# First block issued by a list schedule instead of a fixed table of slots

## Chip, cores and metric

The kernel runs on one core of one Trainium2 chip. The metric is the device time of one execution in microseconds (us). A core has TensorE (PE, products), VectorE (DVE), ScalarE (ACT) and GpSimd (POOL), each with an instruction queue of its own that it works off in order. SyncE (SP) issues nearly all DMA transfers, also in order. An instruction waits at the head of its queue until all that it needs is there.

## What is computed

An attention step in linear form, a gated unit and a second unit follow each other on 4608 tokens (8 batches of 576) of width 512, all in float32:

```
q_s = softmax(q, axis=d);  k_s = softmax(k, axis=s)      # per batch and head
x   = q_s @ (k_s^T @ v)                                  # (4608, 512)
y   = (silu(x @ w_gate) * (x @ w_val)) @ w_out           # d_ff = 1536
h   = y @ w_in;  solu = h * softmax(h)                   # d_ff = 1024
out = layernorm(solu) * g_ln @ w_out2
```

The weights arrive as 64-bit floats and are converted on the chip. Each product of two float32 matrices is made of three products of a high part and a low part (high x high, high x low, low x high).

## The kernel before

Tokens are worked on in nine blocks of 512. In a block the hidden width 1536 is cut into twelve groups n = 0 to 11. A group is a gate product g (12 matmuls, L753 to L755), a value product v (12) and an output product o (12) that adds to four accumulators y. After g comes a silu on ScalarE (L792); after v a multiplication on VectorE (L797), a cast to the high part ah on ScalarE (L800) and a subtraction to the low part al on VectorE (L801). o(n) needs ah and al. Four PSUM banks (gv) turn round among g, v and the small products of attention.

While block j runs, attention for block j+1 is made: row maxima of k (L399), maxima over all rows and subtraction (L411 to L432), exp (L493), k-v products (pk, L502) with reciprocals and two parts (L512 to L520), the q steps (L572 to L590, exp L580), q transposes (pq, L602) and x products (px, L666 to L668) with xh on ScalarE (L671) and xl on VectorE (L673).

The first block also converts all its weights. There are 18 raw tiles: wgv0 to wgv11 (gate and value columns of a group) and wo0 to wo5 (output rows of two groups). A conversion has four parts: two activations on ScalarE (L212, L213), two joins on VectorE (L221, L225), the cast to the high part on ScalarE (L236), and the low part on VectorE (L246). The joined result goes to a scratch tile t. Six raw tiles are loaded early, seven (mid: wgv4, wgv5, wo2, wgv6, wgv7, wo3, wgv8) into memory of the prologue, and the last five (again: wgv9, wo4, wgv10, wgv11, wo5) into slots of earlier weights. For these, the earlier weight must first have been used by its v product and stored to DRAM (stream_store, L258), from where later blocks load it again.

The prologue before the first block (attention of block 0 and the first four conversions) is ordered by a clock of nominal times (KEYS). In the first block, `first_tasks` puts every conversion and attention step at a fixed slot 3n to 3n+2 of the group n, and `block` issues slot after slot, each task with all its parts on all engines. So queues hold conversions in the order of use, one or two per group:

```
at(t, 3 * n, lambda no=no: conv_todo[no].start())
at(t, 3 * n + 2, lambda no=no, home=home: conv_todo[no].join(*home))
```

with the cast in the next group's first slot and the low part in its third. Where two conversions fall in one group, their scratch tiles are t2 and yt of the pool tmp. In the prologue they are two tiles t in the pool att0, whose memory the mid loads reuse. The conversions of blocks 1 to 8 are not there; those blocks reload converted weights.

Of the kernel before, what the change touches and what calls it, by code (L numbers as in the profile page):

```python
# [73 lines left out]
class Clock:  # L74
# [14 lines left out]
    def run(self):  # L89
        while self.todo:  # L90
            self.now, _, task = heappop(self.todo)
            if not task.done:
                d = task.step()
                if not task.done:
                    self.put(self.now + d, task)


def finish(f, *a):
# [3 lines left out]
def need(x):  # L102
    if not x:
        raise ValueError("an order that cannot be")
# [3 lines left out]
def attention_glu_solu_kernel(  # L108
# [46 lines left out]
    def f32(ap):  # L155
        return ap.bitcast(F32)
# [425 lines left out]
    def q_norm(pool, j, hs, eng=nc.gpsimd):  # L582
        qt = qt_t[j][1][:, :, hs, :]
        n, nc_, nh = qt.shape[:3]
        qs = stat.tile([n, nc_, nh, 1], F32, tag="qs", bufs=2, name="qs")
        nc.vector.tensor_reduce(out=qs[:, :, :, 0], in_=qt, axis=AX.X, op=ALU.add)
        nc.vector.tensor_scalar_add(out=qs, in0=qs, scalar1=1e-9)
        nc.vector.reciprocal(out=qs, in_=qs)
        q_step(j, hs, 3)
        eng.tensor_tensor(  # L590
            out=qt, in0=qt, in1=qs.to_broadcast([n, nc_, nh, D]), op=ALU.mult
        )
# [100 lines left out]
    def at(t, g, f, *a):  # L693
        t.setdefault(g, []).append((f, a))
# [52 lines left out]
    def y_of(j):  # L747
        return y_dram[:, :, BLOCKS[j][0]:sum(BLOCKS[j])]
# [46 lines left out]
    def v_rest(j, i, pv):  # L795
        st = acts[j, i]
        nc.vector.tensor_tensor(out=st, in0=st, in1=pv, op=ALU.mult)  # L797
        ah = apool.tile([P, BLOCKS[j][1]], F32R, tag="ah", bufs=2, name="ah")
        al = apool.tile([P, BLOCKS[j][1]], F32R, tag="al", bufs=2, name="al")
        nc.scalar.copy(out=ah, in_=st)  # L800
        nc.vector.tensor_tensor(out=al, in0=st, in1=f32(ah), op=ALU.subtract)  # L801
        acts[j, i] = (ah, al)

# [1 line left out]
        g_rest(j, i, proj("wg", j, i))  # L805

    def emit_v(j, i, *o):
        v_rest(j, i, proj("wv", j, i))
        pend.append((j, i, *o))

    def next_o(lag):
# [3 lines left out]
    def block(j, fs, dst, t, g0=0):  # L815

        r = {}
        for n, i in enumerate(fs):
            at(r, g0 + 3 * n, emit_g, j, i)
            at(r, g0 + 3 * n + 1, next_o, 1)  # L820
            at(r, g0 + 3 * n + 2, emit_v, j, i, n == 0, n == len(fs) - 1, dst)
        for g in sorted(r.keys() | t.keys()):
            for f, a in r.get(g, []) + t.get(g, []):
                finish(f, *a)
# [107 lines left out]
        load_w1(w_b, f"b{n}", *x)  # L932
    nc.sync.dma_start(out=g_sb, in_=g_ln.rearrange("(c p) -> p c", p=P))

    def first_tasks():

        t = {}
        later, first = [], conv_n[0]
        for n in range(NF - 1):
            for w, _, _ in later:
                at(t, 3 * n, w)
            for _, w, f in later:
                at(t, 3 * n + 2, w)
                if f in streamed:
                    at(t, 3 * n + 3, stream_store, f)  # L950
            later = []
            for m in range(2 - n % 2):
                if first == len(order):
                    break
                no, first = first, first + 1
                home = (tmp, ("t2", "yt")[m])
                at(t, 3 * n, lambda no=no: conv_todo[no].start())
                at(t, 3 * n + 2, lambda no=no, home=home: conv_todo[no].join(*home))
                nm, i = order[no]
                later.append((  # L960
                    lambda no=no: conv_todo[no].upper(), lambda no=no: conv_todo[no].rest(),
                    i if nm == "wgv" else None,
                ))
        need(first == len(order) and not later)
        for f in range(3):
            at(t, 0, stream_store, f)
        for n, (x, tag) in enumerate(zip(again, ("a0", "a1", "a3", "a4", "b0"))):
            at(t, 3 * n + 2, load_w1, w_b if tag == "b0" else wpool, tag, *x)
# [5 lines left out]
        for u in range(2):  # L974
            at(t, 20, kv_mm, ps_at, att, 1, 0, u)
        at(t, 21, kv_load, att, 1, HG)
        at(t, 21, v_load, att, 1, HG)
        at(t, 23, q_norm, att, 1, ALLH, nc.vector)
        at(t, 26, x_tiles, ph1x, 1)
        at(t, 29, kv_max_rows, att, 1, HG)  # L980
        at(t, 29, kv_max_all, att, 1, HG, HG)
        at(t, 30, kv_exp, 1, HG)
        for u in range(2):
            at(t, 32, kv_mm, ps_at, att, 1, HG, u)
        for p, (g, x) in enumerate(((26, 29), (27, 30), (30, 33), (31, 34))):
            at(t, g, q_transpose, ps_at, att, 1, p)
            at(t, x, x_mm, ps_at, 1, p)
        at(t, 33, kv_next, 1)
        at(t, 34, q_next, 1)
        for e, f in enumerate(STREAM):  # L990
            if f is not None and e > STREAM.index(None):
                at(t, 3 * f + 2, stream_next, 0, e)
        return t
# [277 lines left out]
```

## Time and profile before

| what | value |
|---|---|
| median of 3 runs | 1436.24 us (1435.14 to 1437.85) |
| the profiled execution | 1435.06 us, its span 1433.3 us |
| TensorE busy in the span | 1373.9 us (96%) |
| VectorE, ScalarE busy | 715.4 us (50%), 647.4 us (45%) |
| mean granted TensorE clock | 0.983 |
| first block (v0 to v11) | about 45 to 188 us |

A span is the time from the first to the last instruction. In a timeline each row gives start and duration; durations of matmuls overlap, so the time that one takes is the distance of starts. A bracket at a row's end gives the idle time of the engine before it and what ended it. A clock of 1.00 is 2.4 GHz, 0.5 is 1.2 GHz. In the list of waits, the engine on the left waited for what stands behind the arrow.

### The profile page before, as it was taken

What the parts mean: (1) busy time and instruction counts of PE and PEld (TensorE: products, weight loads), DVE (VectorE), ACT (ScalarE), POOL (GpSimd) and SP (SyncE); (2) the same over time, 40 slices, a digit from 0 to 9 for tenths busy, and PEclk for the clock granted to TensorE, in tenths of its full rate; (3) what the DMA queues carried; (4) which work ended last, traced back from release to release, by engine and by line L of the source; (5) the groups of instructions that cost most, each with busy time, mean ns of one, the idle gap of its engine ahead of it and who ended that gap; (6) DMA issues with size and microseconds to landing.
All of it is one profiled execution on the core that took longest, in us unless ns stands there. A gap on an engine that the chain in (4) does not pass through costs nothing.

```text
span 1433.3 us, 17363 instructions
## 1 busy us (share of the span) xinstructions
PE 1373.9 (96%) x6829; PEld 1135.1 (79%) x6829; DVE 715.4 (50%) x1227; ACT 647.4 (45%) x885; POOL 126.2 (9%) x106
## 2 busy tenths in 40 slices
PE   7886799999999999999999999999999999999998
PEld 5665588888888888888888888888878888888887
DVE  6776834434434434434444423331257666666663
ACT  4655425425424524524524514321147566566563
POOL 3000002102012012012021011000000000000000
PEclk8998899999999999999999999999999999999999
DMA  9971386475565565654645442562324433443341
GB/s 288 272 273 41 122 203 145 124 198 127 139 189 122 157 170 121 168 162 120 175 161 112 146 168 68 214 232 83 147 61 109 110 96 74 103 103 97 102 77 42
DMA packets 246657, 201.42 MB, mean 141 GB/s; under 512 B 204208, under 2 KB 218544, under 8 KB 234800
## 3 DMA queue, kind: packets, MB, share of 16 engines
q1 hardware_dynamic: 246576, 200.31, 49.9%
q8 instruction: 54, 0.88, 0.3%
q14 instruction: 27, 0.22, 0.1%
HBM read 140.51 MB, written 35.65 MB: 123 GB/s over the span
## 4 chain that ended last, share of the span: by engine, by line
PE 82%; DVE 7%; ACT 6%; SPq 2%; issue 2%; DMA 1%; ACTq 0%; DVEq 0%
PE wg L753 6%; PE wv L753 6%; PE wv L755 6%; PE wv L754 6%; PE y L753 6%; PE y L755 6%; PE y L754 6%; PE wg L754 6%; PE wg L755 6%; PE y L1166 4%; PE y L1165 4%; PE y L1164 4%; PE ph L1054 4%; PE ph L1053 4%; PE ph L1055 4%
## 5 line engine op out<-in xcount | busy, mean ns | idle before, releaser
L797 DVE TENSOR_TENSOR st<-st,wv 128x512 f32<-128x512 f32 x108 | 74.2, 687 | 354.5 <-PE wv L755 325.8
L800 ACT CAST ah<-st 128x512 fp32r<-128x512 f32 x108 | 66.8, 618 | 357.7 <-DVE st L797 357.6
L755 PE MATMUL wg<-xh,wgv 128*128 128x512 f32 x432 | 171.4, 397 | 9.1 <-DVE wgv L246 9.1
L753 PE MATMUL wg<-xh,wgv 128*128 128x512 f32 x432 | 173.2, 401 | 2.3 <-ACT xh L671 2.3
L753 PE MATMUL wv<-xh,wgv 128*128 128x512 f32 x432 | 169.3, 392 | 3.3 <-DVE xl L673 3.3
L754 PE MATMUL wg<-xl,wgv 128*128 128x512 f32 x432 | 170.8, 395 | 0.9 <-DVE xl L673 0.9
L755 PE MATMUL wv<-xh,wgv 128*128 128x512 f32 x432 | 168.9, 391 | 0.0
L754 PE MATMUL wv<-xl,wgv 128*128 128x512 f32 x432 | 168.8, 391 | 0.0
L753 PE MATMUL y<-ah,wo 128*128 128x512 f32 x432 | 168.8, 391 | 0.0
L755 PE MATMUL y<-ah,wo 128*128 128x512 f32 x432 | 168.3, 390 | 0.0
L754 PE MATMUL y<-al,wo 128*128 128x512 f32 x432 | 168.2, 389 | 0.0
L801 DVE TENSOR_TENSOR al<-st,ah 128x512 fp32r<-128x512 f32 x108 | 74.8, 693 | 92.0 <-ACT ah L800 92.0
L1166 PE MATMUL y<-w,zl 128*128 128x512 f32 (+1 forms) x296 | 113.8, 385 | 0.7 <-DVE zl L1135 0.7
L1164 PE MATMUL y<-w,zh 128*128 128x512 f32 (+1 forms) x296 | 113.8, 384 | 0.0
L1165 PE MATMUL y<-w,zh 128*128 128x512 f32 (+1 forms) x296 | 113.6, 384 | 0.0
L1053 PE MATMUL ph<-w,yh 128*128 128x512 f32 x288 | 113.0, 392 | 0.0
L1055 PE MATMUL ph<-w,yl 128*128 128x512 f32 x288 | 112.7, 391 | 0.0
L1054 PE MATMUL ph<-w,yh 128*128 128x512 f32 x288 | 112.6, 391 | 0.0
L755 PEld LDWEIGHTS wg<-xh,wgv 128*128 128x128 f32 x432 | 82.5, 191 | 28.3 <-DVE wgv L246 10.8
L792 ACT ACTIVATE st<-wg 128x512 f32<-128x512 f32 x108 | 64.4, 596 | 89.7 <-PE wg L755 89.4
L753 PEld LDWEIGHTS wg<-xh,wgv 128*128 128x128 f32 x432 | 82.7, 192 | 20.2 <-ACT xh L671 3.0
L753 PEld LDWEIGHTS wv<-xh,wgv 128*128 128x128 f32 x432 | 81.5, 189 | 20.2 <-DVE xl L673 3.5
(240 smaller groups left out, 2291.8 us busy)
## 6 DMA issues: line engine op xcount, KB each, us to landing
wgv<-w_dram SPq DMA_DIRECT2D x64, 1024.0 KB, 5.1
vt<-in_v_dram SPq DMA_DIRECT2D x64, 144.0 KB, 4.7
y_dram<-yt SPq DMA_DIRECT2D x9, 1024.0 KB, 4.4
yr<-y_dram SPq DMA_DIRECT2D x9, 1024.0 KB, 5.2
out_dram<-ot SPq DMA_DIRECT2D x35, 256.0 KB, 2.3
w_dram<-wgv SPq DMA_DIRECT2D x8, 1024.0 KB, 8.7
w_dram<-w2r SPq DMA_DIRECT2D x8, 1024.0 KB, 3.9
w<-w_dram SPq DMA_DIRECT2D x8, 1024.0 KB, 4.8
```

Of the source, the lines that this page charges most:

```text
L753: nc.tensor.matmul(out=po, lhsT=wh, rhs=rh, start=start, stop=False)
L754: nc.tensor.matmul(out=po, lhsT=wh, rhs=rl, start=False, stop=False)
L755: nc.tensor.matmul(out=po, lhsT=wl, rhs=rh, start=False, stop=stop)
L797: nc.vector.tensor_tensor(out=st, in0=st, in1=pv, op=ALU.mult)
L800: nc.scalar.copy(out=ah, in_=st)
L801: nc.vector.tensor_tensor(out=al, in0=st, in1=f32(ah), op=ALU.subtract)
L1053: nc.tensor.matmul(out=po, lhsT=yh[:, kk, s], rhs=wh, start=(kk == 0), stop=False)
L1054: nc.tensor.matmul(out=po, lhsT=yh[:, kk, s], rhs=wl, start=False, stop=False)
L1055: nc.tensor.matmul(out=po, lhsT=yl[:, kk, s], rhs=wh, start=False, stop=(kk == KD - 1))
L1164: nc.tensor.matmul(out=po[:, s], lhsT=zh[:, c, :], rhs=wh[:, s], start=first, stop=False)
L1165: nc.tensor.matmul(out=po[:, s], lhsT=zh[:, c, :], rhs=wl[:, s], start=False, stop=False)
L1166: nc.tensor.matmul(out=po[:, s], lhsT=zl[:, c, :], rhs=wh[:, s], start=False, stop=last)
```

## The change

`first_tasks` and the first call of `block` are replaced by `first_block`, which gives every step of the block to a planner (`Plan`): each task is a list of stages, each with an engine and a nominal time. The planner then simulates the engines on these times and issues a stage when it chooses it. Among the stages that could begin soon it takes that with the longest remaining chain, plus a number per task from a table of some hundred (`plan` in KEYS). A task's parts are now separated by `yield`, so parts of different tasks can interleave, and each conversion stands on its own. Only two conversions stay in the prologue's clock, and all later ones use t2 and yt. The tables say that mid loads land at 0, 2, 5, 12, 16, 23 and 27 us, that a store takes 0.5 us and lands 5 us later, and that a reload takes 1 us and lands 8 us later. Line numbers of the new kernel are higher by about 99.

```diff
     xmm=(23.65, 22.75, 25.3, 26.8),
-    conv=(17.35, 22.1, 26.0, 27.85),
+    conv=(17.35, 22.1),
+    mid=(0, 2, 5, 12, 16, 23, 27),
+    att1=(9, 40),
...
+class Plan:
+    PE, DVE, ACT, SP = 'PE DVE ACT SP'.split()
...
+    def add(self, name, stages, f, *a, after=(), at=0, behind=0, then=()):
...
+    def run(self, sizes):
...
+                    ready.append((begin, -rest((name, t["n"])) - self.first.get(name, 0), name))
+            need(ready)
+            begin, urgent, name = min(ready)
+            eng, us = (left[name]["stages"][left[name]["n"]][k] for k in ("eng", "us"))
+            for b, u, x in sorted(ready):
+                s = left[x]["stages"][left[x]["n"]]
+                if s["eng"] == eng and u < urgent and b < begin + max(us - self.patience, .1):
+                    begin, urgent, name, us = b, u, x, s["us"]
+            t = left[name]
+            s = t["stages"][t["n"]]
+            if s["slot"]:
+                took[s["slot"]].append(name)
+            table = s["table"] or table
+            free[s["eng"]] = begin + s["us"]
+            t["end"].append(begin + s["us"] + s["land"])
+            t["n"] += 1
+            t["task"].step()
...
+        return max(free.values())
...
+        yield d["km"]
...
-    def first_tasks():
...
-                at(t, 3 * n, lambda no=no: conv_todo[no].start())
-                at(t, 3 * n + 2, lambda no=no, home=home: conv_todo[no].join(*home))
...
-        at(t, 5, kv_max_rows, att, 1, 0)
-        at(t, 11, kv_max_all, att, 1, 0, HG)
-        at(t, 17, q_max, att, 1, ALLH, nc.vector)
-        at(t, 18, kv_exp, 1, 0)
-        at(t, 18, q_exp, 1, ALLH)
...
+    def first_block():
+        plan = Plan(*K["plan"])
+        PE, DVE, ACT, SP = plan.PE, plan.DVE, plan.ACT, plan.SP
...
+        def convert(no):
+            w = conv_todo[no]
+            w.start()
+            yield
+            w.join(*homes[turn[0] % 2])
+            turn[0] += 1
+            yield
+            w.upper()
+            yield
+            w.rest()
...
+            if no < 6:
+                after, t0 = (), 0
+            elif no < 13:
+                after, t0 = (), K["mid"][no - 6]
+            else:
+                after, t0 = (f"load{no}",), 0
+            plan.add(
+                f"w{no}", [(ACT, 2.4), (DVE, 2.5, 0, None, "t"), (ACT, 1.05), (DVE, 1.25)],
+                convert, no, after=after, at=t0,
+            )
+        for f in streamed:
+            plan.add(f"store{f}", [(SP, .5, 5)], stream_store, f, after=conv["wgv", f])
...
         for n, (x, tag) in enumerate(zip(again, ("a0", "a1", "a3", "a4", "b0"))):
+            plan.add(
+                f"load{13 + n}", [(SP, 1, 8)], load_w1, w_b if tag == "b0" else wpool, tag, *x,
+                after=(("v%d" % n, 0), f"store{n}"),
+            )
...
+        for n in range(NF):
+            plan.add(
+                f"g{n}", [(PE, 2.72, 0, None, "gv"), (ACT, .6, 0, "silu")], gate, n,
+                after=conv["wgv", n] + (((f"v{n - 1}", 0),) if n else ()) + ((f"v{n - 2}",) if n > 1 else ()),
+            )
+            plan.add(
+                f"v{n}", [(PE, 2.72, 0, None, "gv"), (DVE, .7), (ACT, .65), (DVE, .7)], value, n,
+                after=((f"g{n}", 0),), then=(f"g{n}",) + ((f"o{n - 2}",) if n > 1 else ()),
+            )
+            if n < NF - 1:
+                plan.add(
+                    f"o{n}", [(PE, 2.72)], emit_o, 0, n, n == 0, False, None,
+                    after=(f"v{n}", *conv["wo", n // 2]) + ((f"o{n - 1}",) if n else ()),
+                )
...
+        plan.run(dict(gv=4, t=2))
+        pend.append((0, NF - 1, False, True, y_of(0)))
...
-    block(0, range(NF), y_of(0), first_tasks())
+    first_block()
```

On ScalarE, around the conversion of wgv3 (cast L236 before, L334 now): st are silu results, ah high parts, names with r raw tiles. Before:

```order
L800 CAST ah_604<-st_581 128x512
L792 ACTIVATE st_630<-wg_617 128x512
L236 CAST wgv3_632<-t_609 128x1024
L236 CAST wo1_634<-t_612 128x1024
L212 ACTIVATE wgv4r_528<-wgv4r_528 128x1024
L213 ACTIVATE wgv4r_528<-wgv4r_528,floor_bias_74 128x1024
L800 CAST ah_652<-st_630 128x512
L792 ACTIVATE st_682<-wg_669 128x512
```

Now, at the same cast:

```order
L310 ACTIVATE wgv5r_515<-wgv5r_515 128x1024
L311 ACTIVATE wgv5r_515<-wgv5r_515,floor_bias_74 128x1024
L893 ACTIVATE st_719<-wg_686 128x512
L310 ACTIVATE wgv9r_607<-wgv9r_607 128x1024
L311 ACTIVATE wgv9r_607<-wgv9r_607,floor_bias_74 128x1024
L334 CAST wgv3_745<-t_704 128x1024
L334 CAST wo1_747<-t_724 128x1024
L310 ACTIVATE wgv6r_531<-wgv6r_531 128x1024
L311 ACTIVATE wgv6r_531<-wgv6r_531,floor_bias_74 128x1024
L902 CAST ah_771<-st_719 128x512
L893 ACTIVATE st_787<-wg_750 128x512
```

The starts of wgv5 and wgv9 have moved ahead of the cast of wgv3, and wgv3 is cast after wgv4 and wgv7. On SP, from the first store (w1_dram is where converted weights go) to the load of wgv10, before:

```order
L258 DMA w1_dram_109<-wgv0_408 128x2048
L258 DMA w1_dram_109<-wgv1_494 128x2048
L258 DMA w1_dram_109<-wgv2_514 128x2048
L201 DMA wgv9r_614<-in_moe_w_gate_dram 128x4x256
L201 DMA wgv9r_614<-in_moe_w_val_dram 128x4x256
L201 DMA wo4r_661<-in_moe_w_out_dram 128x2x1024
L258 DMA w1_dram_109<-wgv3_632 128x2048
L201 DMA wgv10r_732<-in_moe_w_gate_dram 128x4x256
L201 DMA wgv10r_732<-in_moe_w_val_dram 128x4x256
```

Now:

```order
L356 DMA w1_dram_109<-wgv0_408 128x2048
L356 DMA w1_dram_109<-wgv1_492 128x2048
L299 DMA wgv9r_607<-in_moe_w_gate_dram 128x4x256
L299 DMA wgv9r_607<-in_moe_w_val_dram 128x4x256
L299 DMA wo4r_636<-in_moe_w_out_dram 128x2x1024
L356 DMA w1_dram_109<-wgv2_626 128x2048
L356 DMA w1_dram_109<-wgv4_671 128x2048
L299 DMA wgv10r_742<-in_moe_w_gate_dram 128x4x256
L299 DMA wgv10r_742<-in_moe_w_val_dram 128x4x256
L356 DMA w1_dram_109<-wgv3_745 128x2048
```

The store of wgv2 has moved behind the loads of wgv9 and wo4, and the store of wgv4 ahead of that of wgv3. On VectorE, the k steps of the next block (m and r are maxima, kt is k) stood between conversions, the second part of them here:

```order
L221 SCALAR_TENSOR_TENSOR wgv6r_547<-wgv6r_547 128x1024
L225 SCALAR_TENSOR_TENSOR t_790<-wgv6r_547 128x1024
L411 TENSOR_REDUCE r_795<-m_663 96x8
L417 COPY r2_797<-r_795 32x8 x3
L419 TENSOR_REDUCE r3_801<-r2_797 32x8
L422 COPY mb_803<-r3_801 32x256 x3
L427 STREAM_TRANSPOSE mt_807<-mb_803 96x256
L432 TENSOR_TENSOR kt_536<-kt_536,mt_807 96x1536
L797 TENSOR_TENSOR st_823<-st_823,wv_843 128x512
```

Now they follow the prologue's last step (xl):

```order
L774 TENSOR_TENSOR xl_156<-y1_494,xh_155 128x512
L497 TENSOR_TENSOR m_628<-kt_520 96x256
L497 TENSOR_TENSOR m_628<-m_628,kt_520 96x256 x4
L509 TENSOR_REDUCE r_638<-m_628 96x8
L515 COPY r2_640<-r_638 32x8 x3
L517 TENSOR_REDUCE r3_644<-r2_640 32x8
L520 COPY mb_646<-r3_644 32x256 x3
L525 STREAM_TRANSPOSE mt_650<-mb_646 96x256
L531 TENSOR_TENSOR kt_520<-kt_520,mt_650 96x1536
L344 TENSOR_TENSOR wgv2_626<-t_592,wgv2_626 128x1024
L898 TENSOR_TENSOR st_655<-st_655,wv_613 128x512
```

They have moved from behind the joins of wgv6 to the block's first place, ahead of wgv2's low part and of the first multiplication.

## Rows read from the trace of the kernel before

**Rows 1.** Stretches: us, busy PE, PEld, DVE, ACT, POOL; clock, DMA share, GB/s
```profile
100.00:120.00 20.00, 9.32 (x34) 7.17 (x33) 15.41 (x13) 11.49 (x12) 0.00 (x0) 0.77 0.00 0
...
45.30:188.30 143.00, 110.17 (x534) 89.30 (x533) 100.04 (x130) 76.48 (x92) 0.29 (x2) 0.88 0.57 172
...
70.00:75.00 5.00, 5.00 (x23) 4.12 (x23) 2.80 (x7) 4.72 (x5) 0.00 (x0) 1.00 1.04 421
```
**Rows 2.** TensorE's waits, 0 to 180 us: total us, times, longest us
```profile
PE pk L502 <- ACT kt L493: 12.5, 1, 12.5
PE wg L755 <- DVE wgv L246: 9.1, 4, 2.9
PE pq L602 <- issue: 7.9, 1, 7.9
PE wv L753 <- DVE xl L673: 3.3, 1, 3.3
```
**Rows 3.** TensorE's timeline: start us, duration us, line, operation, tiles, shape
```profile
125.31 0.63 PE L754 MATMUL wg<-xl,wgv 128*128 128x512 f32 x1
125.73 0.63 PE L755 MATMUL wg<-xh,wgv 128*128 128x512 f32 x1
...
155.94 0.60 PE L602 MATMUL pq<-ident,qt 128*128 128x128 f32 x4
...
161.86 0.19 PE L666 MATMUL px<-qh,kvh 128*128 128x64 f32 x1
...
162.81 0.39 PE L753 MATMUL wg<-xh,wgv 128*128 128x512 f32 x1
...
176.54 1.62 PE L502 MATMUL pk<-vt,kt 96*64 96x65 f32 x48
...
185.56 0.39 PE L753 MATMUL wv<-xh,wgv 128*128 128x512 f32 x1
...
188.28 0.39 PE L753 MATMUL wg<-xh,wgv 128*128 128x512 f32 x1
```
**Rows 4.** ScalarE's and VectorE's timelines around conversions
```profile
42.72 1.23 DVE L246 TENSOR_TENSOR wgv<-t,wgv 128x1024 fp32r<-128x1024 f32 x1 [2.56 <-ACT wgv L236]
...
42.71 0.58 ACT L671 CAST xh<-y 128x512 fp32r<-128x512 f32 x1
...
113.71 1.04 ACT L236 CAST wgv<-t 128x1024 fp32r<-128x1024 f32 x1 [4.99 <-DVE t L225]
114.66 1.12 ACT L212 ACTIVATE wgv9r<-wgv9r 128x1024 f32<-128x1024 f32 x1
...
116.78 1.12 ACT L212 ACTIVATE wo4r<-wo4r 128x1024 f32<-128x1024 f32 x1
...
133.49 1.28 ACT L792 ACT_TABLE_LOAD   x1
```
**Rows 5.** SP's timeline: the issues of stores and of reloaded weights
```profile
64.97 5.45 SPq L258 DMA_DIRECT2D w_dram<-wgv  x3
74.46 0.38 SPq L201 DMA_DIRECT2D wgv9r<-in_moe_w_gate_dram  x1
74.89 1.36 SPq L201 DMA_DIRECT2D wgv9r<-in_moe_w_val_dram  x1
76.98 0.82 SPq L201 DMA_DIRECT2D wo4r<-in_moe_w_out_dram  x1
```
**Rows 6.** SP's waits, 45 to 100 us
```profile
SPq L201 <- DVE wo L246: 3.4, 1, 3.4
```
**Rows 7.** DMA issues from 64, 74 and 80 us on: count, size, us to landing
```profile
w_dram<-wgv SPq DMA_DIRECT2D x1, 1024.0 KB, 9.4
...
wgv9r<-in_moe_w_val_dram SPq DMA_DIRECT2D x1, 512.0 KB, 7.6
...
w_dram<-wgv SPq DMA_DIRECT2D x1, 1024.0 KB, 14.0
...
wgv10r<-in_moe_w_val_dram SPq DMA_DIRECT2D x1, 512.0 KB, 12.3
```

More of the change, by code (lines that the diff above doesn't have):

```diff
@@ L95, in run, with __init__, rest @@
                     self.put(self.now + d, task)
+class Plan:
+    PE, DVE, ACT, SP = 'PE DVE ACT SP'.split()
+    def __init__(self, hop, patience, table, slow, first):
+        self.slow, self.hop, self.patience, self.load, self.first = slow, hop, patience, table, first
+        self.tasks = {}
+    def add(self, name, stages, f, *a, after=(), at=0, behind=0, then=()):
+        stages = [dict(zip(("eng", "us", "land", "table", "slot"), (*s, 0, None, None)[:5])) for s in stages]
+        for s in stages:
+            s["land"] = s["land"] or 0
+            if s["eng"] in (self.DVE, self.ACT):
+                s["us"] *= self.slow
+        self.tasks[name] = dict(
+            stages=stages, task=Task(f, a), after=[(x, None) if isinstance(x, str) else x for x in after],
+            at=at, behind=behind, then=then, n=0, end=[],
+        )
+    def run(self, sizes):
+        tail = {}
+        def rest(key):
+            if key not in tail:
+                name, n = key
+                t = self.tasks[name]
+                last = n == len(t["stages"]) - 1
+                more = [] if last else [(name, n + 1)]
+                more += [
+                    (x, 0) for x, u in self.tasks.items() for y, m in u["after"]
+                    if y == name and (m == n or m is None and last)
+                ]
+                more += [(x, 1) for x, u in self.tasks.items() if last and name in u["then"]]
+                tail[key] = t["stages"][n]["us"] + t["stages"][n]["land"] + max(
+                    [rest(k) for k in more] + [t["behind"]]
+                )
+            return tail[key]
+        free, took, table = {}, {k: [] for k in sizes}, None
+        left = dict(self.tasks)
+        while left:
+            ready = []
+            for name, t in left.items():
+                s = t["stages"][t["n"]]
+                begin = max(free.get(s["eng"], 0), t["at"])
+                before = []
+                if t["n"]:
+                    before.append((name, t["n"] - 1))
+                    if t["n"] == 1:
+                        before += [(x, None) for x in t["then"]]
+                else:
+                    before += t["after"]
+                if s["slot"]:
+                    k = len(took[s["slot"]]) - sizes[s["slot"]]
+                    if k >= 0:
+                        before.append((took[s["slot"]][k], None))
+                for x, m in before:
+                    u = self.tasks[x]
+                    m = len(u["stages"]) - 1 if m is None else m
+                    if m >= u["n"]:
+                        break
+                    hop = 0 if u["stages"][m]["eng"] == s["eng"] else self.hop
+                    begin = max(begin, u["end"][m] + hop)
+                else:
+                    if s["table"] and s["table"] != table:
+                        begin += self.load
+                    ready.append((begin, -rest((name, t["n"])) - self.first.get(name, 0), name))
[7 more added lines that the diff above has]
+            t = left[name]
+            s = t["stages"][t["n"]]
+            if s["slot"]:
+                took[s["slot"]].append(name)
[4 more added lines that the diff above has]
+            t["task"].step()
+            if t["n"] == len(t["stages"]):
+                t["task"].finish()
+                del left[name]
+        return max(free.values())
@@ L807, in emit_v @@
     def emit_v(j, i, *o):
-        v_rest(j, i, proj("wv", j, i))
+        yield from v_rest(j, i, proj("wv", j, i))
         pend.append((j, i, *o))
@@ new lines, in first_block, with gate, value @@
+    def first_block():
+        plan = Plan(*K["plan"])
+        PE, DVE, ACT, SP = plan.PE, plan.DVE, plan.ACT, plan.SP
+        homes = ((tmp, "t2"), (tmp, "yt"))
+        turn = [0]
+        def convert(no):
+            w = conv_todo[no]
+            w.start()
+            yield
+            w.join(*homes[turn[0] % 2])
+            turn[0] += 1
+            yield
+            w.upper()
+            yield
+            w.rest()
+        def gate(n):
+            pg = proj("wg", 0, n)
+            yield
+            g_rest(0, n, pg)
+        def value(n):
+            pv = proj("wv", 0, n)
+            yield
+            yield from v_rest(0, n, pv)
+        conv = {}
+        for no in range(len(order)):
+            nm, i = order[no]
+            conv[nm, i] = ()
+            if no < conv_n[0]:
+                continue
+            conv[nm, i] = (f"w{no}",)
+            if no < 6:
+                after, t0 = (), 0
+            elif no < 13:
+                after, t0 = (), K["mid"][no - 6]
+            else:
+                after, t0 = (f"load{no}",), 0
[5 more added lines that the diff above has]
+            plan.add(f"store{f}", [(SP, .5, 5)], stream_store, f, after=conv["wgv", f])
+        for n, (x, tag) in enumerate(zip(again, ("a0", "a1", "a3", "a4", "b0"))):
+            plan.add(
+                f"load{13 + n}", [(SP, 1, 8)], load_w1, w_b if tag == "b0" else wpool, tag, *x,
+                after=(("v%d" % n, 0), f"store{n}"),
+            )
@@ L990, in first_tasks @@
         for e, f in enumerate(STREAM):
             if f is not None and e > STREAM.index(None):
[L992 to L995 removed]
+                plan.add(f"next{f}", [(SP, .5)], stream_next, 0, e, after=((f"v{f}", 0), f"store{f}"))
+        for n in range(NF):
[6 more added lines that the diff above has]
+                after=((f"g{n}", 0),), then=(f"g{n}",) + ((f"o{n - 2}",) if n > 1 else ()),
+            )
+            if n < NF - 1:
+                plan.add(
+                    f"o{n}", [(PE, 2.72)], emit_o, 0, n, n == 0, False, None,
+                    after=(f"v{n}", *conv["wo", n // 2]) + ((f"o{n - 1}",) if n else ()),
+                )
@@ new lines, in first_block, with load @@
+        for n in range(2):
+            h0 = n * HG
+            if n:
+                def load():
+                    kv_load(att, 1, HG)
+                    v_load(att, 1, HG)
+                plan.add("kvl1", [(SP, 5, 8)], load, after=(("kv0", 0), ("kv1", 0)))
+            plan.add(
+                f"m{n}", [(DVE, 2.25)], kv_max_rows, att, 1, h0,
+                after=("kvl1",) if n else (), at=0 if n else K["att1"][0],
+            )
+            plan.add(f"a{n}", [(DVE, 2.6), (DVE, 1.8)], kv_max_all, att, 1, h0, HG, after=(f"m{n}",))
+            plan.add(f"e{n}", [(ACT, 1.5, 0, "exp")], kv_exp, 1, h0, after=(f"a{n}",))
+            for u in range(2):
+                plan.add(
+                    f"kv{2 * n + u}", [(PE, .8, 0, None, "gv"), (DVE, .35), (ACT, .65), (DVE, .6)],
+                    kv_mm, ps_at, att, 1, h0, u, after=(f"e{n}",),
+                )
@@ new lines, in first_block @@
+        plan.add("qm", [(DVE, 2.3), (DVE, 2.3)], q_max, att, 1, ALLH, nc.vector, at=K["att1"][1])
+        plan.add("qe", [(ACT, 1.95, 0, "exp")], q_exp, 1, ALLH, after=("qm",))
+        plan.add("qn", [(DVE, 2.9), (DVE, 2.3)], q_norm, att, 1, ALLH, nc.vector, after=("qe",))
+        x_tiles(ph1x, 1)
+        for p in range(NPAIR):
+            plan.add(
+                f"t{p}", [(PE, .95, 0, None, "gv"), (ACT, .6), (DVE, .7)], q_transpose, ps_at, att, 1, p,
+                after=("qn",) + ((f"x{p - 2}",) if p > 1 else ()),
+            )
+            plan.add(
+                f"x{p}", [(PE, 1, 0, None, "gv"), (ACT, .6), (DVE, .7)], x_mm, ps_at, 1, p,
+                after=(f"t{p}", f"kv{p}"), behind=8,
+            )
```

44 lines of the change are left out of this document (4 added, 40 removed).

## Prediction

> **What bounds the kernel now.** I read the page's busy shares first. TensorE is at 96% of the span, so over the whole run it is the bound; but the first block of tokens is different, and only that block is changed. There VectorE works 100.0 of 143 us and TensorE's granted clock averages 0.88; in one 20 us slice TensorE is busy for 9.32 us at 0.77 [rows 1]. Next the waits of TensorE: 12.5 us once for the exponential of the next block's k, 9.1 us in four waits for the low part of a converted weight (L246), 7.9 us once before the q transposes, 3.3 us for a last part of x [rows 2]. That is 32.8 us, nearly all between 66 and 174 us. The third view is TensorE's timeline for unit prices: twelve products (one gate, value or output group) take 188.28 - 185.56 = 2.72 us; two k-v groups 1.62 us, so 0.81 each; the transposes of one pair of heads of the next block 0.60 us; one x group 162.81 - 161.86 = 0.95 us [rows 3]. After a long wait the clock stands at 0.5 (1.2 GHz), where products follow at 0.42 us instead of 0.227 [rows 3].
>
> The work of the first block, o10 included, is done 2.72 us after v11: o10 comes after the second block's first gate group, but counted without that group the end is 188.28 + 2.72 = 191.0 us [rows 3]. The changed order puts o10 straight behind the last x group. I predict that end.
>
> **What goes.** In the old order ScalarE and VectorE hold fixed shares of a conversion per group, and their queues put whole attention steps in front of what TensorE needs. In the new order the k steps (m0, a0) stand ahead of nearly all conversions, the exponential runs before TensorE reaches its k-v groups (these now come after o5 and o6 as well), and the q steps stand far ahead of the transposes. By the rows' durations none of the waits in rows 2 comes back at its old place: VectorE's queue after the new wait (below) holds about 73 us of work for 86 us of TensorE's, the 100.0 us of [rows 1] less some 5 us of conversions moved into the prologue and some 22 us done ahead of the wait. So 32.8 us of waits go, and most of the low clock after each.
>
> **What comes: one wait.** On ScalarE the first two instructions of wgv9's conversion now stand ahead of the cast of wgv3, which gate group 3 needs. Conversion no longer follows the order of use, and an engine takes its queue in order. So g3 cannot start before wgv9's raw data has landed, and o0, which is before g3, is TensorE's last work until then.
> How early is that? SP issues the load of wgv9 only when wgv0's store has landed, since both use slot a0. In the old trace: store issued at 64.97, landed 9.4 later, load issued at 74.46 and 74.89, the second half landed 7.6 later, 82.5 us [rows 5, 7]. There it cost nothing, because the conversion began at 114.66 [rows 4]. What shifts it: SP's wait of 3.4 us for wo0's conversion goes [rows 6], because that conversion's scratch tile moved from att0, whose memory wgv7 reuses, to tmp; and the store of wgv2 is no longer ahead of the load. Full profit from the first gives 79.1, none 82.5. The DMA engines are loaded here, so not all of it may come through; I take 79.5. Ends: 76.5 (all of it, and the store's megabyte at 421 GB/s, 2.5 us [rows 1]) and 84.
> ScalarE gets there earlier. Its last cast of the prologue comes some 2.5 us later than now, because five more conversion steps of 1.23 us stand on VectorE ahead of the last part of x, against 2.56 us that it sits idle there now and one such step that already stands there [rows 4]: near 45.5 instead of 42.7. Then come six first halves of conversions at 2.12 us (114.66 to 116.78), three casts at 0.95 (113.71 to 114.66), five steps of 512 columns at 0.58 and a table load of 1.28 [rows 4], 19 to 20 us, and up to 2 us for wgv7's load: 65 to 68. So TensorE waits about 15 us, and all delays before that (the later end of the prologue, wgv7) are hidden under this wait.
> From the landing on: 2.12 + 0.95 + 0.1 us until wgv3's cast is done, and 0.8 us more since the third product needs VectorE's half, which takes 1.23 [rows 4] while two products cover 0.45: g3 starts in effect at 83.5. Then g3 to g11, v3 to v11 and o1 to o10, 28 groups x 2.72 = 76.2; four k-v groups 3.2, four transposes 1.6 (2.4 at most, but products overlap), four x groups 3.8: 84.8 us. One restart at the low clock, some 7 products x 0.2 = 1.4 us. 83.5 + 86.2 = 169.7 us.
> 191.0 - 169.7 = 21.3 us gained. I take off 1.3 us for hand-offs that the rows cannot show in a new order (under half of the smallest wait in rows 2): **20 us**. The second block finds its x, its k and its reloaded weights about as far ahead as now, since their loads are issued after the same groups; the blocks after it are the same instructions, costed at nothing. If the second block's reloads came late, the cost would be one load, about 5 to 8 us.
> The profiled execution took 1435.06 us, 1.76 over its span and 1.18 under the median of the runs. 1435.06 - 20 = 1415.1; against the median, 1416.
>
> A rule bears on the landing. What the row shows: a load issued in a busy stretch lands after 7.6 us, and one store after 9.4, another after 14.0 [rows 7]. The Trainium skill (DMA: Bandwidth & Descriptors, section "Queues, rings and completion order") says that each DMA engine takes descriptors in ring order. By that, the load of wgv9 stands behind all that SP issued before it, and with the third store no longer before it, it would land earlier by that store's megabyte, an estimate of 2.5 us at the pace of the row. By the rule the sum would be 1413.5; I keep the row's time, 1416, since these landings differ among themselves by more.
>
> **Rivals.**
> 1. wgv9 lands before ScalarE gets there (67 or sooner). For it: the order was laid out as if it did, with that conversion before wgv3's. Against: the planner's table gives store and reload 5 and 8 us to land, the rows 9.4 and 7.6 [rows 7], and its SP starts free while the trace's comes to the stores at 64.97 [rows 5]; from 61.6 on, 5 us would have to do for both. Then TensorE's wait shrinks by 12.5 us: gain 32.5, 1404.
> 2. More waits of the same kind. wgv10's load is issued when wgv2's store has landed, and that store now goes out after the loads of wgv9 and wo4, near 74.5 (wo4 is issued at 76.98 now [rows 5], less about 3). Landing 9.4 later, its load 12.3 later [rows 7]: 96 to 97. ScalarE reaches that conversion near 92, and behind it stands the cast that o3 needs; o3 is due at 83.5 + 6 x 2.72 = 99.8, so data after 96 delays TensorE one for one. With a store of 14.0 us it lands near 101: 5 us lost. With small losses on VectorE, whose queue has little slack, the gain falls to 8 to 15: 1421 to 1428, in the middle 1424.
> 3. Slower than before. The reloads become one series: wgv9's landing releases wgv3's conversion, whose store releases wgv11's load; a wait at each of the five reloads (wgv9, wo4, wgv10, wgv11, wo5) at the long prices, 14.0 + 12.3 = 26.3 us a turn from the first store at 61.6 on, ends at 193, and o10 some 9 us later: 202, 11 us late, 1447. For it: SP issues in order, and two of the stores now wait for conversions behind a load. Against: the stores of wgv2 and wgv4 are free early, so the turns overlap. It decides the sign from a last landing at about 182 us on.
> 4. The prologue's tail and the start are late by more than the wait hides (over 12 us): nothing in rows 4 is that large. No gain only if rivals 2 and 4 meet.
>
> **How the numbers follow.** Forecast, a single long wait with a gain of 16 to 24: 0.60. Rival 1: 0.10. Rival 2: 0.20. Rival 3: 0.06. No change: 0.04. A difference of 0.2%, about 3 us, is what a measurement of this kernel can tell. Faster 0.60 + 0.10 + 0.20 = 0.90, same 0.04, slower 0.06. The forecast's own range is 1412 to 1420 (landing 76.5 to 84 moves it 4 up or down). The range to hold 8 times in 10 takes in rival 2 nearly whole and stops short of rival 1's 1404: 1406 to 1427.
>
> **What would show it.** Right: TensorE has one wait of 10 to 20 us, released by wgv3's conversion, with ScalarE idle just before wgv9's first instruction for the load; from there no wait over 3 us to o10; o10's end at 165 to 174 us; later blocks' lengths unchanged. Wrong: ScalarE finds wgv9 there; or TensorE has more waits above 3 us after g3, or the second block begins with one; or the first k-v groups still wait for the exponential.

## Result, and the profile after

The changed kernel takes 1414.76 us, median of 4 runs (1413.32 to 1415.59). The kernel before, run on the same chip, takes 1436.23 (1435.14 to 1437.85). The ratio is 0.9849, with a 95% interval of 0.9831 to 0.9866, so the gain is 21.5 us. The forecast was 1416. The profiled execution took 1413.32 us with a span of 1411.5. That is 21.8 us under the span of before, and all of it lies in the first block, as the end of o10 shows. TensorE's timeline (start us, duration us, line, operation, tiles, shape), which answers to [rows 3]:

```profile
81.17 0.80 PE L854 MATMUL wg<-xh,wgv 128*128 128x512 f32 x1 [10.08 <-ACT wgv L334]
...
84.72 0.63 PE L855 MATMUL wg<-xl,wgv 128*128 128x512 f32 x1
85.15 0.58 PE L856 MATMUL wg<-xh,wgv 128*128 128x512 f32 x1
...
86.28 0.39 PE L854 MATMUL wv<-xh,wgv 128*128 128x512 f32 x1
```

Gate group 3 starts at 81.17 after a wait of 10.08 us. Its products follow at 0.42 us, and value group 3 starts at 86.28. o10's twelve products begin at 166.56 and take 2.72 us, so the block's work ends at 169.28 instead of 191.0 [rows 3]. Behind that end lie 1411.5 - 169.3 = 1242.2 us here and 1433.3 - 191.0 = 1242.3 before: the rest of the program is as long as it was.

TensorE's waits, 48 to 170 us (total us, times, longest us), which answer to [rows 2]:

```profile
PE wg L854 <- ACT wgv L334: 10.1, 1, 10.1
PE y L854 <- ACT ah L902: 1.9, 1, 1.9
PE y L855 <- DVE al L904: 1.8, 1, 1.8
```

The four old waits, 32.8 us, are gone. One new long wait stands in their place, and two short ones in o0. Stretches (us, busy PE, PEld, DVE, ACT, POOL; clock, DMA share, GB/s), which answer to [rows 1]:

```profile
100.00:120.00 20.00, 20.00 (x90) 16.57 (x89) 18.75 (x19) 12.41 (x16) 0.00 (x0) 1.00 0.27 106
48.00:78.00 30.00, 19.33 (x73) 14.73 (x71) 21.68 (x30) 18.37 (x20) 0.00 (x0) 0.78 1.10 305
78.00:169.30 91.30, 88.10 (x473) 72.54 (x474) 73.79 (x97) 57.10 (x70) 0.28 (x2) 0.96 0.54 163
70.00:75.00 5.00, 1.09 (x3) 0.33 (x1) 3.00 (x3) 0.00 (x0) 0.00 (x0) 0.50 0.96 379
```

The slice from 100 to 120 us, where TensorE was busy for 9.32 us at 0.77, is now full at 1.00. What is left of the idle time lies ahead of 81 us: 10.7 of the 30 us from 48 to 78, in which the DMA share is 1.10. From 78 us on VectorE works 73.8 us.

The chain of work that ended last, 48 to 82 us (start us, us, what), gives the reason for the wait:

```profile
49.62 8.89 DMA wgv7r<-in_moe_w_val_dram
58.53 1.01 SPq L655
59.64 1.48 SPq L299
...
62.33 0.81 SPq L1036
63.18 9.06 DMA w_dram<-wgv
72.72 5.18 DMA wgv9r<-in_moe_w_val_dram
78.00 1.10 ACT wgv9r L310
79.10 1.08 ACT wgv9r L311
80.18 0.94 ACT wgv L334
81.17 0.80 PE wg L854
```

Read it from the bottom. Gate group 3 waits for the cast of wgv3 (L334). That stands on ScalarE behind the two first instructions of wgv9's conversion (L310, L311). These wait for wgv9's data, which the load brings only after wgv0's store has landed and cleared the slot, and SP comes to that store at 63.18, behind q's eight loads (L655), wo3, wgv8 and g_sb. ScalarE's timeline confirms it (the bracket is its idle time and what ended it), and shows the second reload, which makes nobody wait:

```profile
68.91 0.63 ACT L893 ACTIVATE st<-wg 128x512 f32<-128x512 f32 x1
78.00 1.10 ACT L310 ACTIVATE wgv9r<-wgv9r 128x1024 f32<-128x1024 f32 x1 [8.47 <-DMA wgv9r<-in_moe_w_val_dram]
...
92.19 1.19 ACT L310 ACTIVATE wgv10r<-wgv10r 128x1024 f32<-128x1024 f32 x1
```

One more pair of views tells what the old stall was made of. These are VectorE's and ScalarE's waits, 48 to 192 us, in the kernel before:

```profile
ACT wgv L236 <- DVE t L225: 31.7, 8, 5.0
DVE al L801 <- ACT ah L800: 27.3, 12, 5.3
```

And in the kernel after, 48 to 170 us:

```profile
DVE al L904 <- ACT ah L902: 2.5, 2, 2.2
...
ACT wgv L334 <- DVE t L323: 1.8, 1, 1.8
```

Before, the two engines waited for each other in both directions. ScalarE's high part of a value group (ah) stood behind the first halves of the next conversions, so VectorE waited for ah 12 times. Then ScalarE's cast stood behind VectorE's joined weight t, which VectorE reached only after that wait. After, both waits are nearly gone.

### The profile page after: what moved, and what is told of

It is laid out like the page before. It is cut to its first block, busy times and chain, and to the rows that moved or that the text cites. A ratio compares the mean times of both kernels' runs of the same rounds, so it can differ in the third digit from the quotient of the medians.

```text
span 1411.5 us, 17346 instructions
## 1 busy us (share of the span) xinstructions
PE 1370.0 (97%) x6829; PEld 1132.6 (80%) x6829; DVE 714.0 (51%) x1227; ACT 648.4 (46%) x885; POOL 126.2 (9%) x106
## 4 chain that ended last, share of the span: by engine, by line
PE 88%; ACT 4%; DVE 4%; DMA 2%; SPq 1%; issue 1%; POOL 0%; ACTq 0%; DVEq 0%
PE wg L854 7%; PE y L854 6%; PE y L856 6%; PE y L855 6%; PE wg L856 6%; PE wg L855 6%; PE wv L854 6%; PE wv L856 6%; PE wv L855 6%; PE y L1316 4%; PE y L1315 4%; PE y L1314 4%; PE ph L1204 4%; PE ph L1203 4%; PE ph L1205 4%; PE pk L601 2%
## 5 line engine op out<-in xcount | busy, mean ns | idle before, releaser
L854 PE MATMUL wg<-xh,wgv 128*128 128x512 f32 x432 | 171.7, 398 | 10.8 <-ACT wgv L334 10.1
L855 PE MATMUL wg<-xl,wgv 128*128 128x512 f32 x432 | 169.7, 393 | 0.3 <-DVE xl L774 0.3
L854 PEld LDWEIGHTS wg<-xh,wgv 128*128 128x128 f32 x432 | 81.9, 190 | 28.8 <-ACT wgv L334 10.8
L855 PEld LDWEIGHTS y<-al,wo 128*128 128x128 f32 x432 | 81.6, 189 | 19.0 <-DVE al L904 2.2
L854 PEld LDWEIGHTS y<-ah,wo 128*128 128x128 f32 x432 | 81.5, 189 | 19.0 <-ACT ah L902 2.3
```

What stands on the lines that cost most here:

```text
L854: nc.tensor.matmul(out=po, lhsT=wh, rhs=rh, start=start, stop=False)
L855: nc.tensor.matmul(out=po, lhsT=wh, rhs=rl, start=False, stop=False)
```

## Experiments

My theory had two parts. The gain comes from the end of this hand-over, and what is left of the stall is the one wait for wgv9. Rivals: the gain is due to the new places of the second block's attention, or to the two conversions that left the prologue; and the wait for wgv9 hides others of its size. The experiments ran in three groups, each beside the kernel before (1434.37, 1436.14 and 1435.78 us); times of different groups are compared through their ratios to it. A profile is of one execution only, and need not be near the median.

**Where the gain comes from.** First the kernel before, with one edit:

```diff
-                at(t, 3 * n, lambda no=no: conv_todo[no].start())
+                at(t, 3 * n + 2, lambda no=no: conv_todo[no].start())
```

> The kernel before with one thing changed: the first two ScalarE instructions of every conversion are issued two slots later, behind the value group's high part (ah) and just ahead of VectorE's joining step, instead of in front of the gate group. No list schedule; attention and casts where they were; four conversions in the prologue as before. Theory A (the stall in the kernel before is a hand-over in both directions: VectorE waits 27.3 us in 12 waits for ah, which stands on ScalarE behind the next conversions' starts, and ScalarE 31.7 us in 8 waits for VectorE's joined weight; a few instructions at the right place undo most of it): 10 to 15 us of the gain come by this alone, 1421 to 1426 us. Theory B (it is the new places of the second block's attention that pay): no gain, 1433 to 1437.

Measured: 1422.25 us, ratio 0.9913 (0.9899 to 0.9926), 12.1 us gained by the medians; the two profiled spans differ by 15.4, all of it ahead of value group 11, which starts at 170.2 instead of 185.6. VectorE's and ScalarE's waits for each other and TensorE's, 48 to 192 us:

```profile
ACT ah L800 <- DVE st L797: 26.7, 9, 5.6
DVE al L801 <- ACT ah L800: 12.5, 13, 1.9
...
ACT wgv L236 <- DVE t L225: 11.3, 4, 2.8
...
PE pk L502 <- ACT kt L493: 8.2, 1, 8.2
...
PE pq L602 <- issue: 6.6, 1, 6.6
...
PE wv L753 <- DVE xl L673: 3.3, 1, 3.3
...
PE wg L755 <- DVE wgv L246: 2.8, 2, 2.5
```

Theory A held. Both hand-over waits more than halve, 59.0 to 23.8 us together. ScalarE now idles in front of ah instead (26.7 us in 9 waits for st), as it has to be free when VectorE's st comes; TensorE's four waits of [rows 2] still fall from 32.8 to 20.9 us together. Next the attention alone:

```diff
-        at(t, 17, q_max, att, 1, ALLH, nc.vector)
-        at(t, 18, kv_exp, 1, 0)
-        at(t, 18, q_exp, 1, ALLH)
+        at(t, 14, q_max, att, 1, ALLH, nc.vector)
+        at(t, 15, kv_exp, 1, 0)
+        at(t, 15, q_exp, 1, ALLH)
...
-        at(t, 23, q_norm, att, 1, ALLH, nc.vector)
+        at(t, 20, q_norm, att, 1, ALLH, nc.vector)
```

> The kernel before with the second block's attention alone issued earlier: maximum over q from slot 17 to 14, both exponentials from 18 to 15, q's normalisation from 23 to 20. Conversions where they were. Theory A (hand-over between VectorE and ScalarE): TensorE's wait of 12.5 us for the exponential of k gets shorter, but others grow by as much, since the two engines do not get through the queue sooner: 1434 to 1438 us. Theory B (the attention's places are the gain): the 12.5 and the 7.9 us go for the most part, 1418 to 1426 us.

Measured: 1433.76 us, ratio 0.999 (0.9981 to 0.9999), so no difference or hardly one. The waits, 48 to 192 us:

```profile
ACT wgv L236 <- DVE t L225: 32.3, 8, 5.0
DVE al L801 <- ACT ah L800: 28.6, 12, 5.3
...
PE wg L753 <- DVE kvl L520: 7.9, 1, 7.9
...
PE px L667 <- DVE ql L613: 6.0, 1, 6.0
...
PE pk L502 <- ACT kt L493: 1.3, 1, 1.3
```

TensorE's 12.5 us for the exponential of k fell to 1.3, but waits of 7.9 and 6.0 came at other places. The hand-over between the two engines stayed as it was, and so did the time. Then both edits together:

> The kernel before with both hand edits: the conversions' first ScalarE instructions two slots later, and the second block's attention steps three slots earlier. Theory A (the attention's places gave nothing alone because the hand-over hid them; with that gone, the remaining waits of 8.2 us for the exponential of k and 6.6 us before the q transposes shrink): 1415 to 1420 us. Theory B (they only move): 1420 to 1425, as with the starts alone.

Measured: 1417.14 us, ratio 0.9867 (0.9853 to 0.988), 18.6 us gained. By the medians Theory A held: with the hand-over mended, the attention's places are worth another 0.0046 of 1,436 us, 6.6 us (0.9913 to 0.9867), where alone they were worth at most 2.7 (0.9981). How much it is stays open, though: the profiled executions, the fastest of four with the first edit alone and the slowest of four with both, are only 1.2 us apart (spans 1417.9 and 1416.7). TensorE's longest wait is now 4.9 us, and its wait for the exponential of k is nearly gone (48 to 192 us):

```profile
DVE al L801 <- ACT ah L800: 11.7, 13, 1.9
...
PE wg L753 <- ACT st L792: 4.9, 1, 4.9
...
PE pk L502 <- ACT kt L493: 1.1, 1, 1.1
```

So two hand edits of five places, without any planner, give 18.6 of the planner's 21.5 us by the medians, and 16.6 of 21.8 by the profiled spans. What the rest is due to (the other places of the planner's order, SP's order, the scratch tile that left att0) was not tried one by one.

The two conversions that left the prologue were tried twice. First put back, with everything planned anew:

```diff
-    conv=(17.35, 22.1),
+    conv=(17.35, 22.1, 26.0, 27.85),
```

> The changed kernel with four conversions in the prologue, as before the change, instead of two; the other conversions are planned by the same list schedule. Theory A (the gain lies in the block's order; the two conversions moved are work that has to be done in either place and is hidden in either): within 3 us of the changed kernel, 1413 to 1418. Theory B (moving conversions out of the prologue, so that the first block starts sooner, is a large part of the gain): 1422 to 1428.

Measured: 1426.63 us, ratio 0.9934 (0.9922 to 0.9946). By the number theory B would hold, but TensorE's waits, 48 to 185 us, are new ones:

```profile
PE y L854 <- ACT ah L902: 14.8, 1, 14.8
PE wg L854 <- ACT st L893: 12.0, 1, 12.0
```

With two tasks fewer the planner had laid out another order. That left the cause open, so the next run, with the edit above as well, kept the order and moved the work alone:

```diff
         def convert(no):
+            if no < 4:
+                yield
+                yield
+                yield
+                return
...
-            if no < conv_n[0]:
+            if no < 2:
```

> The changed kernel with the conversions of the third and fourth weight done in the prologue, at the places where the kernel before has them; unlike in the run with four conversions before (1426.6), the planner still plans these two, as steps that issue nothing, so that all other instructions keep the changed kernel's order. Theory A (that run was slow because its order came out different and worse: output group 0 and the gate behind it waited 14.8 and 12.0 us): work only moves from one side of 46 us to the other and the wait for wgv9 hides the rest, 1411 to 1417 us. Theory B (two conversions in the prologue are themselves worth it): 1421 to 1428.

Measured: 1413.86 us, ratio 0.9847 (0.9833 to 0.986), the changed kernel's. Theory A held: where these two conversions are done is worth nothing here, and the 12 us of the run before are the order's. It is worth nothing in this order, in which the wait for wgv9 (10.3 us in this run) comes after them and hides what they cost; an order without that wait was not tried.

**What is left.** The store of wgv0 ahead of q's loads (the planner's own store of wgv0 then issues nothing, by an edit of one more line):

```diff
         if n == 5:
+            stream_store(0)
             q_next(0)
...
```

> The changed kernel with one store moved: wgv0's goes out on SP ahead of the eight loads of q (issued from 50.4 us on) instead of behind them (63.2). The order on the compute engines is that of the changed kernel. Theory A (what is left of the stall is one chain: wgv0's store, 9.1 us, then wgv9's load, 5.2 us, then ScalarE's first instruction of that conversion): q's loads and all behind them go out 2 us later, the load of wgv9 is then issued at about 67.5 us instead of 72.3 because SP gets there only then, its data land at 73 to 75 instead of 77.9, and TensorE's wait for the cast of wgv3 falls from 10.1 to 5.5 to 7.5 us: 1410 to 1412 us, against 1414.8. Theory B (the wait is there anyway, released by something else just behind, or the later q loads eat it): 1414 to 1416.

Measured: 1413.61 us, ratio 0.9854 (0.9839 to 0.9869), the changed kernel's and a little under Theory B's range. Theory A failed, and SP's timeline and the landing (count, size, us from issue) tell where:

```profile
69.75 0.38 SPq L299 DMA_DIRECT2D wgv9r<-in_moe_w_gate_dram  x1
70.18 1.70 SPq L299 DMA_DIRECT2D wgv9r<-in_moe_w_val_dram  x1
```

```profile
wgv9r<-in_moe_w_val_dram SPq DMA_DIRECT2D x1, 512.0 KB, 7.9
```

The load went out 2.5 us sooner (70.18 against 72.72) and took 7.9 us instead of 5.2, so ScalarE began at 78.14 instead of 78.00, and TensorE's wait was 11.7 us. The same transfers had been issued ahead of it. For these to be fewer, q's loads have to come later:

```diff
         if n == 5:
-            q_next(0)
+            stream_store(0)
...
+        def load_q(*a):
+            load_w1(*a)
+            q_next(0)
...
-                f"load{13 + n}", [(SP, 1, 8)], load_w1, w_b if tag == "b0" else wpool, tag, *x,
+                f"load{13 + n}", [(SP, 1, 8)], load_w1 if n else load_q, w_b if tag == "b0" else wpool, tag, *x,
```

> The changed kernel with SP's queue rearranged and the compute engines' order as it was: wgv0's store goes out right after the loads of wgv7, and the eight loads of q (1 MB in small rows, 9 to 11 us to issue) go out behind the load of wgv9 instead of 20 us ahead of it. In the run with the early store alone the load of wgv9 went out 2.5 us sooner and landed no sooner (78.1 against 77.9), so what sets the landing is the transfers ahead of it and not the issue. Theory A (that, and the wait for wgv9 is the last thing that delays the rest of the old order): wgv9 lands at 66 to 70, ScalarE finds it, TensorE's wait of 10.1 us falls under 3, q lands near 80 and costs VectorE 3 us at most: block 6 to 9 us shorter, 1405 to 1409 us. Theory B (as with the late conversion, the time comes back as waits for VectorE's and ScalarE's queue): 1412 to 1416.

Measured: 1409.76 us, ratio 0.9816 (0.9803 to 0.983). ScalarE's timeline:

```profile
74.23 1.10 ACT L310 ACTIVATE wgv9r<-wgv9r 128x1024 f32<-128x1024 f32 x1 [4.18 <-issue]
```

It lies between the two theories. The data came 3.8 us sooner, not 8 to 12: SP spent 4.75 us on the 4 KB load g_sb and 3.30 on a store ahead of this load, and the load took 9.3 us. Of the 3.8 us TensorE kept 2.8 at the end of o10 (166.5 against 169.28). The span is 4.5 us shorter; the other 1.7 arise near 1,020 us, where nothing was edited. There TensorE waits 2.96 us in every run. In the changed kernel the products after that wait follow at 0.43 us (granted clock 0.66 from 1020 to 1025 us), here at 0.23 (1.00). From the end of that wait the program takes 391.1 to 391.4 us in ten of the fourteen profiled executions, both kernels' among them, and 389.6 to 389.7 in four; what decides between the two was not found, and nothing shows that this edit did. Next the planner was told the real starts of the reloaded weights, so that wgv9 no longer stands ahead of wgv3's cast:

```diff
-                after=(("v%d" % n, 0), f"store{n}"),
+                after=(("v%d" % n, 0), f"store{n}"), at=(27, 31, 40, 49, 55)[n],
```

> The changed kernel; only its planner is told when the five reloaded weights can really start to be converted (27, 31, 40, 49, 55 us after its start, from the landings in the trace of the changed kernel), so that it lays wgv9's conversion behind the casts that are needed first. Theory A (the planner counted SP as free and the landings as short, and put a conversion that had to wait for a load ahead of the cast of wgv3): TensorE's wait of 10.1 us before gate group 3 goes, o10 ends 6 to 8 us earlier, 1407 to 1409 us. Theory B (VectorE and ScalarE have no room left, and the wait only moves to other groups): within 2 us of the changed kernel, 1413 to 1417.

Measured: 1413.06 us, ratio 0.9853 (0.984 to 0.9867). Theory B held. TensorE's waits, 48 to 170 us:

```profile
PE wg L856 <- DVE wgv L344: 4.4, 2, 3.6
PE y L854 <- ACT ah L902: 2.9, 1, 2.9
PE y L855 <- DVE al L904: 1.8, 1, 1.8
PE wg L854 <- ACT wgv L334: 1.6, 1, 1.6
```

The wait of 10.1 us is gone and gate group 3 starts at 73.94 instead of 81.17. But gate group 6 takes from 106.2 to 114.2, with a wait of 3.6 for the low part of its weight and slow products after it. The block's work ends at 169.45, as late as before the edit. VectorE's timeline names what stands ahead of that low part (L344 at 109.15): q's normalisation, 5.1 us, which this order puts between the weight's cast and its low part.

```profile
104.01 2.29 DVE L686 TENSOR_REDUCE qs<-qt 128x32 f32<-128x2048 f32 x1
...
106.94 2.29 DVE L691 TENSOR_TENSOR qt<-qt,qs 128x2048 f32<-128x2048 f32 x1
109.15 1.22 DVE L344 TENSOR_TENSOR wgv<-t,wgv 128x1024 fp32r<-128x1024 f32 x1
```

The planner laid out the whole block anew here (the second block's first k-v products start at 98.95 instead of 124.54), so this run does not tell what wgv9's conversion moved by itself, with all else in its place, would give. With q's loads moved as well:

> The planner with realistic starts of the reloaded weights together with q's loads behind the load of wgv9. With the realistic starts alone (1413.1) the wait before gate group 3 was gone, and a wait for the low part of wgv6 before gate group 6 had come in its place. Theory A (that one too hangs on late data): 1405 to 1410 us. Theory B (it is VectorE's queue, which is no shorter): 1411 to 1415.

Measured: 1413.3 us, ratio 0.9845 (0.9831 to 0.9858). Theory B: the new wait does not hang on the landing. ScalarE now finds wgv9 there, and the wait of 3.7 us before gate group 6 stays, behind the same steps on VectorE.

Last, two other tables for the planner, only numbers changed (the entry of wgv9's conversion is w13; nearly all other entries differ too):

```diff
-    'w13': -20,
+    'w13': -420,
```

> The changed kernel with other numbers in the table that breaks ties among ready steps; all else as it was. The numbers come from a search against a replay of the block with durations and landings from the traces, which gives o10's end 20 us earlier than for the changed kernel's table (147 against 167). Theory A (the order still has slack that a better table finds, among others the place of the reloaded weights' conversions): 1395 to 1404 us. Theory B (the search fits the replay and not the chip; the changed kernel's block is bound by VectorE's and ScalarE's queues whatever the order): 1410 to 1418.

Measured: 1424.72 us, ratio 0.9926 (0.9912 to 0.9939): slower than the changed kernel by some 11 us, worse than either theory said. TensorE's waits, 48 to 185 us:

```profile
PE y L854 <- ACT ah L902: 12.1, 2, 10.9
PE pk L601 <- ACT kt L592: 10.0, 1, 10.0
```

> As the run before, with the numbers of another search (o10's end 17 us earlier in the replay). Theory A: 1397 to 1407 us. Theory B: 1410 to 1418.

Measured: 1408.91 us, ratio 0.9815 (0.9802 to 0.9829), the lowest median of all. Here wgv9's entry is -300. The replay had set this table 3 us behind the other; the chip sets it 16 ahead. So an order can be better, but a replay of this kind does not tell which. With q's loads moved:

> The second searched table together with the SP order in which q's loads go out behind the load of wgv9. Theory A (both shorten waits that follow one another): 1402 to 1406 us. Theory B (in the searched order the compute queues are the limit, the landing is hidden there): 1408 to 1412.

Measured: 1410.44 us, ratio 0.9822 (0.9808 to 0.9835). Theory B by the medians: nothing on top. Two versions (q's loads moved, and this table alone) thus beat both kernels, by some 5 us over the changed one; their intervals just do not meet its own. The profiled executions say less: up to the wait near 1,020 us they gain 24.6 us (q's loads moved), 23.0 (this table) and 25.6 (both) over the kernel before, against 21.7 for the changed kernel.

## Why the prediction was right

**The end of the block.** Predicted 169.7 us, measured 169.28. Gain in the profile 21.8, predicted 21.3 before the 1.3 taken off for hand-offs.

**What goes.** That all of [rows 2] would go was right. The reason given, shares of a conversion per group and whole attention steps in front of what TensorE needs, was half right: attention steps moved alone gave a ratio of 0.999, and more only once the hand-over was mended. What holds TensorE up for the larger part (12.1 of the 21.5 us by the medians) is the place of the conversions' first halves in ScalarE's queue, ahead of ah. The prediction did not name it; rows 2 names only the last link of each chain.

**The one wait.** Place and releaser were right; the terms were off by 1 to 5 us, in part against each other. The landing came 1.6 us sooner than predicted, the way from it to gate group 3 took 0.3 longer and the gaps behind took 0.9: that the end of the block came out within 0.4 us is in part luck.
- Issue of the load: 72.72 instead of the old 74.89 [rows 5]. Of SP's 3.4 us [rows 6] 2.2 came through. The prediction let an earlier issue bring an earlier landing; the experiment with the early store shows that by itself it does not.
- Landing: 77.9, predicted 79.5 (76.5 to 84). The load took 5.2 us, where [rows 7] has 7.6.
- ScalarE there: 69.5 (78.00 - 8.47), predicted 65 to 68; it had waited 3.1 us for wgv7.
- TensorE's wait: 10.1, predicted 15. The later ScalarE does not enter it, since the landing decides. It is shorter because o0 ended later (it had waits of 1.9 and 1.8 us and ran at the low clock) and the data came sooner.
- Start of gate group 3 in effect: 86.28 - 2.72 = 83.56, predicted 83.5 and 1.4 for the clock, so 1.3 sooner. From there 85.7 us to the end; the prediction's groups and steps sum to 84.8, and 0.9 us of small gaps came on top.

The Trainium skill (DMA: Bandwidth & Descriptors, section "Queues, rings and completion order") says that a DMA engine takes its descriptors in the order of the ring. The traces agree: with one store fewer ahead, the load took 2.4 us less than in [rows 7], near the estimate of 2.5; issued 2.5 us sooner behind the same transfers, it landed no sooner. The size is loose: with two stores just ahead of it in SP's queue the load took 4.9 to 7.3 us in four runs, with three 7.4 to 8.4 in five, with four 9.8 in one. The sum by the rule was 1413.5, by the row 1416; the median lies between.

**Rivals.** 1, early landing, failed: ScalarE sat idle for 8.47 us. 2, further waits of the kind, did not come, by a hair: wgv10's data landed at 85.20 + 6.4 = 91.6, and ScalarE took them at 92.19. 3 and 4 did not come; the reloads overlap, and the second block starts without a wait.

**What the prediction did not say** is what taking the wait away would give. It counted the landing as moving the end one for one. In the same order that nearly held for 3.8 us (2.8 kept). In the planner's other order the wait went and its time came back within 40 us, but at steps which that order had placed anew; what the wait is worth by itself is not shown.

## What to carry to other kernels

When two engines hand work to each other, list their waits for each other in both directions before those of the engine that sets the time: here a step that nobody waited for yet, queued ahead of one that somebody did, made both engines wait. The first two instructions of every conversion, moved behind the urgent one, gave 12 of 21 us. When an order is planned from nominal times, look in its trace for an in-order engine that stands idle for a transfer with ready work behind it, and measure what its removal gives before counting on it: where the planner lays out everything anew, other waits change too.

## What was not expected of the hardware

Between 48 and 78 us the DMA engines' share is about 1, and there the time at which SP issues a load does not set its landing by itself: issued at 70.18, 72.72 and 64.85 us the same 512 KB landed 7.9, 5.2 and 9.3 us later. In that stretch SP's issue of a 4 KB load took 4.75 us in one run and 0.81 in another. After the wait of 10.08 us in the changed kernel, in which the granted clock is 0.50 (1.2 GHz, 70 to 75 us), products follow at 0.42 us until 85.15 and then at 0.23. After the wait of 2.96 us near 1,020 us the clock falls in ten of the fourteen profiled executions and not in four.
